# A convolution and two-layer MLP kernel: another layout for two early parts of x, the first convolution by token halves, four VectorE taps ahead of the weight copies, and moved slots of the second product

## The chip, the cores and the metric

The kernel runs on one core of a Trainium2 chip. The metric is the device time of one execution in microseconds. Beside the time there is one profiled execution with a trace of every engine: TensorE (PE, with its weight loads as PEld), VectorE (DVE), ScalarE (ACT), GpSimd (POOL, which also issues DMAs), and SyncE (SP, which issues DMAs).

## The reference

```python
# x (8, 4096, 192), weight (8, 7), w_in (192, 2048), w_out (2048, 192), all float32
w = softmax(weight, axis=-1)                       # 7 taps for each of 8 heads of 24 channels
y[b, s, c] = sum_k w[head(c), k] * x[b, s - 6 + k, c]      # causal, zeros before s = 0
h = y.reshape(32768, 192) @ w_in
out = maximum(0.01 * h, h) @ w_out
```

## The kernel before

**Layout.** Two of the eight sequences are worked on together (e = 0 and 1). Their channels lie on the partitions, 64 channels of one sequence on partitions 0 to 63 and the same 64 of the other on 64 to 127; 192 channels are three such chunks c = 0, 1, 2. Tokens run along the free dimension. The work goes through `groups`: four half groups of 256 tokens (two blocks of 512, each in two halves), then 30 groups of 512 tokens. Of x, the first 1024 tokens of the first two sequences come in four special parts q = 0 to 3 of 256 tokens; the parts 1 and 2 (`x_rows`, loaded at L145) lie token by token on the partitions, two tokens a partition, token s*128+p as slot s of partition p. TensorE transposes them (`transpose_first`, L167) into one bf16 PSUM tile `t[p, s, c, k]`, and VectorE copies that to the transposed input `xt` (`evac_first`, L195), one copy for each s, 384 elements a partition. Everything after comes by DMA and a DMA transpose.

**The convolution.** For most groups VectorE does it: a first tap at L222 and six multiply-adds at L228 for each chunk, 21 instructions in all (`conv_jobs`). The first group's convolution, and chunks 0 and 2 of the second group's, are matmuls with diagonal weights (`pe_conv_jobs`, L259): the taps as two bf16 parts p = 0 and 1, so 14 jobs a chunk with a matmul for each e, 64 rows by 64 columns of the array. With `cross` the two sequences land on exchanged PSUM halves, so that a crossed chunk and an uncrossed one use different quarters of the array, and four matmuls run at once. `evac` multiplies by the reciprocal of the softmax sum (`rsum`) and brings the result to `yt`; a crossed one takes two instructions of 64 partitions. The diagonals `diag[c][:, p]` are made by VectorE (L420) in the order (0,0), (0,1), (1,0), (2,0), (1,1), (2,1).

In the kernel before, the first group's chunk 0 is split by the parts of the taps: part 0 into `hi`, part 1, crossed, into `low`, which ScalarE scales (L455), and one VectorE instruction (L465) adds both.

**The two products.** `mm1` (L507) is called for u = 0, 1, ...; each call makes one PSUM tile `ph` of 128 by 1024 (two feature chunks of a half group, or one of a 512 group, for both sequences) and a ScalarE Prelu (L515) that writes `g`. There are two `ph` tiles. A half group has eight u in four steps j, a 512 group sixteen in eight steps. In the very first u, chunk 0's and chunk 1's matmuls come first, then the transposes of part 1, then chunk 2's. `w_in` exists on the partitions in two arrangements; `spread_down` (L322) and `spread_up` (L326) copy 64 partitions to the other 64 once a piece has landed, since each sequence needs all weights on its own partitions. Its second half (`w_in[1]`) is needed from u = 4 of the first group on.

The second product of the four half groups is done in **row slots** (`mm2_row_slot`, L525), 256 of them. A pair of output tiles of 128 tokens takes 32 slots in two rounds of 16. A slot is two matmuls, one on each half of the array's rows; in the second round the halves change places. Between the rounds stands a **seal**: at the last slot of the first round ScalarE copies out the other tile of the pair before (`evac_o`, L638), after that round's last matmul, and the first matmuls of the second round wait for this copy:

```python
            if first and rnd == 1:
                sync(ins, seal, "both row tiles have left these banks")
        if last and rnd == 0:
            seal_round(p, ins)
        if last and rnd == 1:
            evac_o(pair[0])
```

With slot number q, q = 16, 48, 80, ... wait for a seal, and q = 32, 64, ... do not.

**What orders the work.** The schedule is written by hand: each engine does its instructions in program order. `plan` says how many row slots follow the two u of each step j of group i, and `between` how many of them are put ahead of the second u (0 ahead of the first and 4 ahead of the second, in the steps listed). Behind the last half group's step 7 the 512 groups use another form of the second product (L588). `CUTS` says behind which u of the first group the second group's convolution matmuls go. VectorE convolves group i+1 while group i is in the products.

Of the kernel before, what the change touches and what calls it, by code (L numbers as in the profile page):

```python
# [10 lines left out]
FP32 = mybir.dt.float32  # L11
# [4 lines left out]
def kernel(  # L16
# [8 lines left out]
    nc = tc.nc  # L25
# [11 lines left out]
    NCH = D // CH  # L37
    ST = 512
    SUB = ST // 128
    HT = ST // 2  # L40
    HS = SUB // 2
# [8 lines left out]
    for k in range(K):  # L50
        SKEW += [(2, k), next(pair)]
    SKEW += [(1, 5), (0, 6), (1, 6)]
    CUTS = {1: (0, 6), 3: (6, 11), 5: (11, 14)}
    GB = 32
    NR = D // (2 * GB)

    const_pool = ctx.enter_context(tc.tile_pool(name="const", bufs=1))
# [14 lines left out]
    groups = [(b, h * HT, HT) for b in range(NHALF) for h in range(2)]  # L72
# [49 lines left out]
    def new_xt(rp):  # L122
# [10 lines left out]
    x_rows = {  # L133
        q: const_pool.tile([128, 2, HS, D], BF16, name=f"x_rows{q}") for q in (1, 2)
    }

    def load_first(q):
        rows = x[0:2, q * HT : (q + 1) * HT, :].rearrange("e (s p) d -> p e s d", s=HS)
        if q == 0:
            x_nat[q] = stage_pool.tile([128, 2, HS, D], FP32, name="x_nat")  # L140
            for s in range(HS):
                nc.sync.dma_start(out=x_nat[q][:, :, s], in_=rows[:, :, s])
        elif q in x_rows:
            for e in range(2):
                nc.gpsimd.dma_start(out=x_rows[q][:, e], in_=rows[:, e])  # L145
        else:
            for c in range(NCH):
                for e in range(2):
                    nc.gpsimd.dma_start(  # L149
                        out=x_half[q][:, c, :, e, :],  # L150
                        in_=rows[:, e, :, c * CH : (c + 1) * CH],
                    )
# [7 lines left out]
    ptr = {}  # L160

    def transpose_first(q, mid=None):
        if q:
            t = psum_o.tile([128, HS, NCH, 128], BF16, name="ptr", tag="po")
            for s, c in product(range(HS), range(NCH)):
                for e in range(2):
                    nc.tensor.transpose(  # L167
                        out=t[e * CH : (e + 1) * CH, s, c, :],
                        in_=x_rows[q][:, e, s, c * CH : (c + 1) * CH],
                        identity=ident,  # L170
                    )
            ptr[q] = [t[:, s] for s in range(HS)]
            return
        ts = [
            psum_o.tile([128, NCH, 128], FP32, name=f"ptr{s}", tag="po") for s in range(HS)
        ]
        for s, t in enumerate(ts):
            if s and mid is not None:
                mid()
            for c in range(NCH):  # L180
                nc.tensor.matmul(
                    out=t[:, c, :],
                    lhsT=x_half[q][:, c, s, :, :].rearrange("p e k -> p (e k)"),
                    rhs=ident,
                    start=True,
                    stop=True,
                )
        ptr[q] = ts

    def evac_first(q, *copies):  # L190
        dst = xt[0][:, :, HALO + q * HT : HALO + (q + 1) * HT]
        dst = dst.rearrange("p c (s k) -> p s c k", s=HS)
        for s, t in enumerate(ptr.pop(q)):
            for cs in (slice(0, 1), slice(1, NCH)) if q == 0 and s else (slice(0, NCH),):
                copies[s](out=dst[:, s, cs], in_=t[:, cs])  # L195

    def transpose_half(q):
# [37 lines left out]
    def y_of(grp, c):  # L235
        blk, t0, T = grp
        if blk not in yt:
            yt[blk] = yt_pool.tile([128, NCH, ST], BF16, name="yt")
        return yt[blk][:, c, t0 : t0 + T]

    def acc_tile():
        return psum_o.tile([128, ST], FP32, name="acc", tag="po")
# [37 lines left out]
    def run(*lists):  # L280
        for slots in zip_longest(*lists, fillvalue=()):
            for both in slots:
                for job in both:
                    job()
# [27 lines left out]
    near, far = slice(0, WF // 2), slice(WF // 2, WF)  # L312
# [8 lines left out]
    def spread_down(n, copy=nc.vector.tensor_copy, cols=slice(0, WF)):  # L321
        copy(out=w_in[n][0:CH, 1, cols], in_=w_in[n][CH:128, 0, cols])  # L322

    def spread_up(n, slots=slice(0, 3, 2), cols=slice(0, WF)):
        to = slice(slots.start // 2 + 1, (slots.stop - 1) // 2 + 2)
        nc.vector.tensor_copy(out=w_in[n][CH:128, to, cols], in_=w_in[n][0:CH, slots, cols])  # L326
# [121 lines left out]
    load_x(2)  # L448
    diag_wide(1, 1)
    diag_wide(2, 1)  # L450
    spread_up(0, slice(0, 1), near)
    spread_down(0, cols=near)

    def act_scale(out, in_, scale):
        nc.scalar.activation(  # L455
            out=out, in_=in_, func=mybir.ActivationFunctionType.Copy, scale=scale
        )

    hi = acc_tile()
    low = const_pool.tile([128, HT], FP32, name="low")  # L460
    pe_hi, _ = pe_conv_jobs(groups[0], 0, parts=(0,), accs=[hi] * 2)
    pe_lo, evac_lo = pe_conv_jobs(groups[0], 0, cross=True, parts=(1,))
    run(pe_hi, pe_lo)
    evac_lo(act_scale, act_scale, out=low)
    nc.vector.scalar_tensor_tensor(  # L465
        out=y_of(groups[0], 0), in0=hi[:, :HT], scalar=rsum[:, 0, :], in1=low,
        op0=mybir.AluOpType.mult, op1=mybir.AluOpType.add,
    )
    spread_up(0, slice(2, 3), near)
    pe_1, evac_1 = pe_conv_jobs(groups[0], 1)  # L470
    pe_2, evac_2 = pe_conv_jobs(groups[0], 2, cross=True, accs=[acc_tile(), wps[:, 0]])
# [1 line left out]
    evac_1(act_scale)  # L473
    evac_2(nc.vector.tensor_scalar_mul, act_scale)
    spread_up(0, slice(0, 1), far)
    spread_down(0, nc.scalar.copy, far)


    g, po, acc2, osb, seal = {}, {}, {}, {}, None
# [151 lines left out]
    def evac_o(n):  # L631
# [18 lines left out]
    plan = {  # L650
        0: [0] * 4,
        NSW - 2: [16, 8, 8, 16],
        NSW - 1: [8, 8, 16, 16],
        NSW: [16, 8, 8, 16, 8, 8, 16, 16],
    }
    between = {(1, 0): (3, 5)}
    for i, js in ((NSW - 2, (2, 3)), (NSW - 1, (1, 2)), (NSW, (2, 3, 5, 6))):
        between.update({(i, j): (0, 4) for j in js})
    slot = 0

# [9 lines left out]
    for i, grp in enumerate(groups):  # L670
        blk, t0, T = grp
        steps = T // 64
        if t0 == 0:
            g[blk] = g_pool.tile([128, NFC, 2, ST], BF16, name="g", tag="g")
        quota = plan.get(i, [16] * 4 if T == HT else [5, 5, 6, 5, 5, 6, 8, 8])

        if i == 0:
            ahead = []
        else:
            ahead = conv_jobs(groups[i + 1]) if i + 1 < len(groups) else []  # L680
        per = -(-len(ahead) // steps)
        for j in range(steps):
            early = between.get((i, j), (0, 0))
            for u in range(2 * j, 2 * j + 2):
                mm2_slots(i, early[u % 2])
                mm1(grp, u, 128 if i <= NSW else CH)
                if i == 0 and u == 0:
                    evac_first(1, nc.vector.tensor_copy, nc.vector.tensor_copy)
                    spread_up(0, slice(2, 3), far)
                    conv_1 = conv_jobs(groups[1], (1,))  # L690
                    run([conv_1[:3]])
                    spread_down(1)
                    spread_up(1, slice(0, 1), near)
                    spread_up(1, slice(2, 3))
                    run([conv_1[3:5]])
                    spread_up(1, slice(0, 1), far)
                    run([conv_1[5:]])
                    pe_0, evac_0 = pe_conv_jobs(groups[1], 0)
                    pe_2, evac_2 = pe_conv_jobs(groups[1], 2, cross=True)
                if i == 0 and u in CUTS:  # L700
                    cut = slice(*CUTS[u])
                    run(pe_0[cut], pe_2[cut])
                if i == 0 and u == 5:
                    evac_0(nc.vector.tensor_scalar_mul)
                    evac_2(nc.vector.tensor_scalar_mul, nc.vector.tensor_scalar_mul)
                if i == 0 and u == 6:
                    transpose_first(2)
                    evac_first(2, nc.vector.tensor_copy, nc.vector.tensor_copy)
            jobs = ahead[per * j : per * (j + 1)]
            if T == ST:  # L710


                jobs = ahead[len(ahead) * j // steps : len(ahead) * (j + 1) // steps]
                for job in jobs:
                    job()
                jobs = []
            mm2_slots(i, quota[j] - sum(early))
            if i == 1 and j == 1:
                load_x(3, transpose_x(2))
            for job in jobs:  # L720
                job()
            if i == 0 and j == 3:
                transpose_half(3)

            last_half = t0 + T == ST
            if i == NSW and j == steps - 1:
                evac_o(LAST - 1)
                slot = NSW * NR * NFC
            if j == steps // 4 and last_half and blk > 0:
                load_x(blk + 3)  # L730
            if j == steps // 2 and last_half and blk > 0:
                transpose_x(blk + 2)
# [35 lines left out]
```

## Time and profile before

| | |
|---|---|
| median of 3 runs | 681.26 us (680.83 to 681.55) |
| the profiled execution, first to last instruction | 679.2 us |
| the median less that span | 2.06 us |
| granted TensorE clock, mean of the core | 1.000 |
| VectorE busy, ScalarE busy | 481.2 us (71%), 517.6 us (76%) |
| DMA, mean over the span | 78 GB/s |

The first 17 us are a start-up, in which DMAs, diagonals, copies of weights and the first convolutions must come before products can run. From 17 to 64 us the half groups run with row slots, from there the 512 groups, and 128 matmuls of the last group end the program. In the timeline a row gives the start, the time to the end of the last instruction in it, and the group; matmuls overlap, so the time from one row's start to the next row's start is what a block took. Times below count from the first instruction.

### The profile page before, as it was taken

The page shows a single profiled execution, that of the slowest core. Times are in us where ns is not written, and L with a number is a line of the kernel's source. Part 1 is how long each engine was busy: PE and PEld are TensorE (multiplying, and loading weights), DVE is VectorE, ACT ScalarE, POOL GpSimd, SP SyncE. Part 2 cuts the span into 40 slices and gives each one's busy share as a digit, 9 for nine tenths or more (in the row PEclk, how much of TensorE's full clock was granted, in tenths as well). Part 3 has the DMA queues.
Part 4 walks back from the last instruction along what each step waited for, and adds up shares of the span by engine and source line. Part 5 has one row for each costly group of instructions (what it writes and reads, how often), then busy time and mean ns, then how long its engine had stood idle before and what let it go on. Part 6 is the DMA issues. An engine that isn't in the chain of part 4 may idle for free.

```text
span 679.2 us, 27092 instructions
## 1 busy us (share of the span) xinstructions
PE 674.9 (99%) x12442; PEld 446.3 (66%) x12442; DVE 481.2 (71%) x816; ACT 517.6 (76%) x601; POOL 147.4 (22%) x208
## 2 busy tenths in 40 slices
PE   9999999999999999999999999999999999999998
PEld 6997666666666666666666666666666666666667
DVE  7989477866768766778667687667786676876612
ACT  7899877777787777777777777778777777777781
POOL 8455221122211222211222112222022220000000
PEclk9999999999999999999999999999999999999999
DMA  9999755655737656556556566567365573321123
GB/s 149 99 119 104 52 85 83 84 64 67 96 74 93 76 54 86 84 85 86 66 63 92 80 92 78 56 83 94 73 87 69 60 96 71 72 56 33 34 49 94
DMA packets 213970, 53.27 MB, mean 78 GB/s; under 512 B 209312, under 2 KB 213536, under 8 KB 213856
## 3 DMA queue, kind: packets, MB, share of 16 engines
q0 software_dynamic: 98832, 13.97, 30.3%
q1 hardware_dynamic: 115008, 37.57, 28.0%
q8 instruction: 97, 1.59, 0.9%
q14 instruction: 17, 0.14, 0.1%
q10 hardware_dynamic: 16, 0.00, 0.0%
HBM read 28.31 MB, written 25.17 MB: 79 GB/s over the span
## 4 chain that ended last, share of the span: by engine, by line
PE 98%; DVE 1%; ACT 0%; issue 0%; ACTq 0%
PE ph L507 49%; PE acc L588 44%; PE po L525 5%; PE acc L259 0%; DVE diag L420 0%; PE ptr L167 0%; ACT L366 0%; ACTq L288 0%; DVE w_in L322 0%; DVE yt L465 0%; DVE o_sb L638 0%; DVE x_half L155 0%; ACT w L372 0%; DVE w_in L326 0%; ACT junk L366 0%
## 5 line engine op out<-in xcount | busy, mean ns | idle before, releaser
L515 ACT ACTIVATE g<-ph 128x1024 bf16<-128x1024 f32 x512 | 496.6, 1021 | 139.8 <-PE ph L507 139.6
L228 DVE SCALAR_TENSOR_TENSOR yt<-xt,wk,yt 128x512 bf16<-128x512 bf16 (+1 forms) x582 | 380.1, 715 | 0.2
L507 PE MATMUL ph<-yt,w_in 64*64 64x512 bf16 (+2 forms) x6048 | 377.5, 369 | 0.3 <-DVE yt L465 0.3
L588 PE MATMUL acc<-g,w_out 64*64 64x512 bf16 x5568 | 339.9, 376 | 0.0
L507 PEld LDWEIGHTS <-w_in 64*64 64x64 bf16 (+1 forms) x6048 | 229.7, 131 | 103.4 <-issue 1.1
L588 PEld LDWEIGHTS <-w_out 64*64 64x64 bf16 x5568 | 178.2, 118 | 118.8
L96 POOL DMA_DIRECT2D x_bf<-in_x_dram x180 | 133.9, 774 | 407.6 <-DMA xt<-x_bf 405.6
L610 DVE STREAM_TRANSPOSE o_t<-acc 128x512 f32<-128x512 f32 x87 | 72.9, 875 | 182.2 <-PE acc L588 182.2
L525 PE MATMUL po<-w_out,g 64*128 64x192 bf16 (+1 forms) x640 | 36.8, 243 | 0.0
L525 PEld LDWEIGHTS <-g 64*128 64x128 bf16 (+1 forms) x640 | 32.6, 95 | 3.2 <-issue 0.4
L222 DVE TENSOR_SCALAR yt<-xt,wk 128x512 bf16<-128x512 bf16 (+1 forms) x97 | 28.8, 320 | 2.4 <-DMA xt<-x_bf 2.4
L598 ACT COPY junk<-junk 128x1 f32<-128x1 f32 x58 | 11.1, 191 | 4.1
L638 DVE COPY o_sb<-po 128x192 f32<-128x192 f32 x8 | 2.8, 356 | 6.8 <-PE po L525 3.9
L638 ACT COPY o_sb<-po 128x192 f32<-128x192 f32 x16 | 5.1, 323 | 0.3
L259 PE MATMUL acc<-xt,diag 64*64 64x256 bf16 x126 | 4.7, 272 | 0.1
L149 POOL DMA_DIRECT2D x_half<-in_x_dram x6 | 4.3, 732 | 0.9 <-DMA w_in<-in_moe_w_in_dram 0.9
L259 PEld LDWEIGHTS <-diag 64*64 64x64 bf16 x140 | 3.7, 106 | 1.0 <-issue 0.4
L360 PE MATMUL warm<-const-bfloat16-1.0 128*128 128x512 bf16 (+2 forms) x8 | 3.3, 577 | 0.8 <-PEq L752 0.8
L145 POOL DMA_DIRECT2D x_rows<-in_x_dram x4 | 2.9, 746 | 0.0
L316 POOL DMA_DIRECT2D w_in<-in_moe_w_in_dram x5 | 2.9, 593 | 0.0
L360 PEld LDWEIGHTS <-const-bfloat16-1.0 128*128 128x128 bf16 x10 | 1.2, 128 | 2.2 <-issue 2.2
L326 DVE COPY w_in<-w_in 64x512 bf16<-64x512 bf16 (+1 forms) x7 | 2.3, 337 | 0.2
(52 smaller groups left out, 25.9 us busy)
## 6 DMA issues: line engine op xcount, KB each, us to landing
out_dram<-o_t SPq DMA_DIRECT2D x112, 192.0 KB, 4.7
x_bf<-in_x_dram POOLq DMA_DIRECT2D x180, 64.0 KB, 3.1
out_dram<-o_sb SPq DMA_DIRECT2D x8, 192.0 KB, 2.8
xt<-x_bf SPq DMA_TRANSPOSE x90, 3.2
w_out<-in_moe_w_out_dram POOLq DMA_DIRECT2D x2, 384.0 KB, 8.3
out_dram<-o_t SPq DMA_DIRECT2D x8, 96.0 KB, 2.4
out_dram<-o_sb SPq DMA_DIRECT2D x8, 96.0 KB, 1.7
w_in<-in_moe_w_in_dram POOLq DMA_DIRECT2D x2, 256.0 KB, 5.5
```

Source lines behind the costliest of these rows:

```text
L96: ins = nc.gpsimd.dma_start(out=t[:, c, :, e, :], in_=src[2 * rp + e, :, :, c * CH : (c + 1) * CH],)
L222: lambda s=src, d=dst, c=c: nc.vector.tensor_scalar_mul(d, s, wk[:, c, 0:1])
L228: lambda s=src, d=dst, c=c, k=k: nc.vector.scalar_tensor_tensor(out=d, in0=s, scalar=wk[:, c, k : k + 1], in1=d, op0=mybir.AluOpType.mult, ...
L259: lambda k=k, p=p, a=a, ps=ps, to=to, acc=accs[e]: nc.tensor.matmul(out=acc[to, :T], lhsT=diag[c][ps, p, k, :], rhs=xt[0][ps, c, a : a + T ...
L360: nc.tensor.matmul(out=to[:, 0:cols], lhsT=ones[:, 0:128], rhs=ones[:, 0:cols], start=True, stop=True,)
L507: nc.tensor.matmul(out=ph[m : m + M, e, i * T : (i + 1) * T], lhsT=w_in_of(f, e, c, m, m + M), rhs=y[ps, c, t0 : t0 + T], start=(c == chun ...
L515: act = nc.scalar.activation(out=g[blk][:, nf * u : nf * (u + 1), :, t0 : t0 + T], in_=ph.rearrange("p e (i t) -> p i e t", i=nf), func=my ...
L525: return nc.tensor.matmul(out=po[m], lhsT=g[b][ps, fc, e, s * 128 : (s + 1) * 128], rhs=w_out[ps, fc, :], start=start, stop=stop,)
L588: ins = nc.tensor.matmul(out=acc2[gi, r][e * CH : (e + 1) * CH, 0:T], lhsT=w_out_of(ps, fc, r), rhs=g[b][ps, fc, e, t0 : t0 + T], start=fi ...
L598: seal = nc.scalar.copy(out=junk, in_=junk)
L610: nc.vector.transpose(out=osb[gi, 0][:, 0 : T // GB, :, r], in_=acc2.pop((gi, r))[:, 0:T].rearrange("p (j k) -> p j k", k=GB),)
L638: ins = copy(out=o_sb[:, n % 2, :], in_=po.pop(n))
```

## The change

The loads of parts 1 and 2 of x put tokens 2p and 2p+1 on partition p, so that one row of 1536 bytes is fetched for a partition and sequence, where two of 768 bytes were. The PSUM tile keeps its form, and its copy to `xt` reads the slots s as the innermost dimension, chunk 1 first (256 elements), then chunks 0 and 2 (512 elements).

The first group's chunk 0 is convolved in two halves of 128 tokens, both parts of the taps in each, the second half crossed. ScalarE alone brings both to `yt`. The copies of `w_in` come behind in program order, and the copy at the last `spread_down(0, ...)` goes from ScalarE to VectorE.

In the first group VectorE does four taps of the second group's chunk 1 ahead of the copies of `w_in[1]` where it did three; a fifth and a sixth are placed between those copies, and the seventh after the evacuation of chunk 0. The third cut of convolution matmuls and the evacuations come behind u = 4, where they came behind u = 5.

Eight row slots go from group 4 (the first 512 group) to group 3, and `plan` and `between` are set anew for both.

```diff
-    CUTS = {1: (0, 6), 3: (6, 11), 5: (11, 14)}
+    CUTS = {1: (0, 6), 3: (6, 11), 4: (11, 14)}
...
     def load_first(q):
         rows = x[0:2, q * HT : (q + 1) * HT, :].rearrange("e (s p) d -> p e s d", s=HS)
+        if q in x_rows:
+            rows = x[0:2, q * HT : (q + 1) * HT, :].rearrange("e (p s) d -> p e s d", s=HS)
...
     def evac_first(q, *copies):
         dst = xt[0][:, :, HALO + q * HT : HALO + (q + 1) * HT]
+        if q:
+            dst = dst.rearrange("p c (k s) -> p c k s", s=HS)
+            t = ptr.pop(q).rearrange("p s c k -> p c k s")
+            for copy, cs in zip(copies, (slice(1, 2), slice(0, NCH, 2))):
+                copy(out=dst[:, cs], in_=t[:, cs])
+            return
...
-    spread_up(0, slice(0, 1), near)
-    spread_down(0, cols=near)
...
-    hi = acc_tile()
-    low = const_pool.tile([128, HT], FP32, name="low")
-    pe_hi, _ = pe_conv_jobs(groups[0], 0, parts=(0,), accs=[hi] * 2)
-    pe_lo, evac_lo = pe_conv_jobs(groups[0], 0, cross=True, parts=(1,))
-    run(pe_hi, pe_lo)
-    evac_lo(act_scale, act_scale, out=low)
-    nc.vector.scalar_tensor_tensor(
-        out=y_of(groups[0], 0), in0=hi[:, :HT], scalar=rsum[:, 0, :], in1=low,
-        op0=mybir.AluOpType.mult, op1=mybir.AluOpType.add,
-    )
+    blk, t0, T = groups[0]
+    pe_a, evac_a = pe_conv_jobs((blk, t0, T // 2), 0)
+    pe_b, evac_b = pe_conv_jobs((blk, t0 + T // 2, T // 2), 0, cross=True)
+    run(pe_a, pe_b)
+    evac_a(act_scale)
+    evac_b(act_scale, act_scale)
+    spread_up(0, slice(0, 1), near)
+    spread_down(0, cols=near)
     spread_up(0, slice(2, 3), near)
...
     spread_up(0, slice(0, 1), far)
-    spread_down(0, nc.scalar.copy, far)
+    spread_down(0, cols=far)
...
         NSW - 2: [16, 8, 8, 16],
-        NSW - 1: [8, 8, 16, 16],
-        NSW: [16, 8, 8, 16, 8, 8, 16, 16],
+        NSW - 1: [16, 16, 16, 8],
+        NSW: [8, 16, 8, 8, 16, 8, 8, 16],
...
-    for i, js in ((NSW - 2, (2, 3)), (NSW - 1, (1, 2)), (NSW, (2, 3, 5, 6))):
+    for i, js in ((NSW - 2, (2, 3)), (NSW, (0, 1, 3, 4, 6, 7))):
         between.update({(i, j): (0, 4) for j in js})
...
                     conv_1 = conv_jobs(groups[1], (1,))
-                    run([conv_1[:3]])
+                    run([conv_1[:4]])
                     spread_down(1)
                     spread_up(1, slice(0, 1), near)
                     spread_up(1, slice(2, 3))
-                    run([conv_1[3:5]])
+                    run([conv_1[4:5]])
                     spread_up(1, slice(0, 1), far)
-                    run([conv_1[5:]])
+                    run([conv_1[5:6]])
...
-                if i == 0 and u == 5:
+                if i == 0 and u == 4:
                     evac_0(nc.vector.tensor_scalar_mul)
+                    run([conv_1[6:]])
                     evac_2(nc.vector.tensor_scalar_mul, nc.vector.tensor_scalar_mul)
```

More of the change, by code (lines that the diff above doesn't have):

```diff
@@ L171, in transpose_first @@
                     )
-            ptr[q] = [t[:, s] for s in range(HS)]
+            ptr[q] = t
             return
@@ L191, in evac_first @@
         dst = xt[0][:, :, HALO + q * HT : HALO + (q + 1) * HT]
+        if q:
[4 more added lines that the diff above has]
+            return
         dst = dst.rearrange("p c (s k) -> p s c k", s=HS)
         for s, t in enumerate(ptr.pop(q)):
-            for cs in (slice(0, 1), slice(1, NCH)) if q == 0 and s else (slice(0, NCH),):
+            for cs in (slice(0, 1), slice(1, NCH)) if s else (slice(0, NCH),):
                 copies[s](out=dst[:, s, cs], in_=t[:, cs])
```

## The prediction

> **What bounds the kernel now.** I read the page's busy times and chain first, then the waits of TensorE, then the timelines of single stretches.
>
> ```profile
> PE 674.9 (99%) x12442; PEld 446.3 (66%) x12442; DVE 481.2 (71%) x816; ACT 517.6 (76%) x601; POOL 147.4 (22%) x208
> PE 98%; DVE 1%; ACT 0%; issue 0%; ACTq 0%
> ```
>
> TensorE carries the chain; ScalarE and VectorE have a quarter of the span free. Busy time can hide stalls, so I compare block lengths. Two u and 16 slots of a half group take 2.63 us (rows at 19.75, 22.38, 25.01, 27.64), the same each time; six L507 matmuls of 512 columns always take 0.65 and eight slot matmuls 0.33. The view of waits lists none for TensorE from 17 to 63 us. So **from 17 us on TensorE has no slack to give back**: a stall there goes into the time in full, and a gain can only come from before. There the waits are small: from 4 to 17 us I count 2.7 us beyond the pace of the columns (a 256-column group of four matmuls every 0.109 us); nearly half is the change between forms of the array, 0.12 to 0.13 a change, and the diff changes their number by none.
>
> This is a stretch of group 4 with its row slots, TensorE and then ScalarE (start, length, group):
>
> ```profile
> 50.61 0.81 PE L507 MATMUL ph<-yt,w_in 64*128 64x512 bf16 x6
> 51.26 0.50 PE L525 MATMUL po<-w_out,g 64*128 64x192 bf16 x8
> 51.59 0.81 PE L507 MATMUL ph<-yt,w_in 64*128 64x512 bf16 x6
> 52.24 0.49 PE L525 MATMUL po<-w_out,g 64*128 64x192 bf16 x8
> 52.57 0.81 PE L507 MATMUL ph<-yt,w_in 64*128 64x512 bf16 x6
> 53.22 0.50 PE L525 MATMUL po<-w_out,g 64*128 64x192 bf16 x8
> 53.55 0.81 PE L507 MATMUL ph<-yt,w_in 64*128 64x512 bf16 x6
> ```
>
> ```profile
> 49.51 3.96 ACT L515 ACTIVATE g<-ph 128x1024 bf16<-128x1024 f32 x4 [0.33 <-PE ph L507]
> 53.37 0.31 ACT L638 COPY o_sb<-po 128x192 f32<-128x192 f32 x1
> 53.56 1.96 ACT L515 ACTIVATE g<-ph 128x1024 bf16<-128x1024 f32 x2
> ```
>
> See the order on ScalarE. A step "u, 4 slots, u, 4 slots" ends on TensorE at 52.57. Its last Prelu still runs then, so the `evac_o` copy behind it runs from 53.37 to 53.68: **0.80 to 1.11 us after the slots ended**. Today that costs nothing: 52.57 is q = 192, a pair's end (192 = 6 x 32), and nobody waits for that copy soon.
>
> **Moved slots.** Summing the old plan, steps end at q = 112, 144, 176, 208 and 240 (odd multiples of 16, where the next slot waits for the seal) only behind 12 or 16 slots, and two whole u follow: 1.30 us of cover. Q = 176 shows it: slots end at 48.66, the copy runs 48.87 to 49.18, slots go on at 49.95. In the new plan group 3 ends at q = 168. Group 4 then goes u, 4, u, 4 and is at 176; u, 4, u, 12 to 192; u, u, 8 to 200; u, 4, u, 4 to 208; u, 4, u, 12 to 224; u, u, 8 to 232; u, 4, u, 4 to 240; u, 4, u, 12 to 256. So the three seals at 176, 208 and 240 stand behind the short block of 4 slots, and **only one u (0.65 us) stands between a seal and the slots that wait for it**. The steps ahead (u, u, 8, then u, 4, u, 4) are those of the fence, so the copy ends 1.11 us after the block; 0.05 us passes from a ScalarE end to a matmul that waited (5.10 to 5.15). The stall is 1.11 + 0.05 - 0.65 = 0.51 us, three times: **+1.53 us**. Queued behind the waiting matmul on TensorE are 4 slots, a u and 12 slots; ScalarE, the one that could catch up, is not the bound. Bounds: 0.8 us in all if the Prelu ahead starts 0.25 us sooner each time, 1.8 if the weight load also waits (0.1 each). VectorE's convolution of group 4 ends at 46.16, just when group 4 begins (46.04); eight slots more in group 3 move that need 0.66 us later, which covers VectorE's new lateness below. SP's transposes of the next block stand behind an output DMA that comes a step sooner; VectorE waited 1.67 us for them at 47.82 and will wait less, and none of that is on the path.
>
> **Chunk 0 by halves.** It goes from 28 matmuls of 256 columns to 56 of 128: 14 groups of four. Nearest row: the transposes (L167), 12 matmuls of 128 columns in 0.46 us, a pair every 0.055, each with 64 weight columns. So 14 x 0.056 = 0.78 us, as long as now (5.15 to 5.93); slow end, one group for each 0.106 us weight load of L259: 1.5 us, 0.6 late for all behind. I take the fast end: the transposes load weights at that pace. [...]
> Two ScalarE instructions (0.95) and one on VectorE (0.48) go; three on ScalarE come. L455 takes 0.47 for 256 columns, and 128 columns fewer are 0.11 less (L195 on ScalarE: 0.48, 0.38, 0.27 for 384, 256, 128), so 3 x 0.37 from 6.14, when `rsum` is there: chunk 0 is ready at 7.25, where it was at 8.04. What is late next is chunk 1:
>
> ```profile
> 7.70 0.47 ACT L455 ACTIVATE yt<-acc,rsum 128x256 bf16<-128x256 f32 x1 [0.49 <-PE acc L259]
> 8.20 0.47 ACT L455 ACTIVATE yt<-wps,rsum 64x256 bf16<-64x256 f32 x1
> 8.70 0.62 ACT L322 COPY w_in<-w_in 64x512 bf16<-64x512 bf16 x1
> ```
>
> Its matmuls wait for the diagonal (2,0), done at 5.97, in both kernels, so they still end at 7.65 and this row still runs 7.70 to 8.18. Chunk 0's products start at 7.70 instead of 8.09, but chunk 1's at 8.23 instead of 8.31: **only 0.08 us won**. ScalarE's weight copy (0.62) goes to VectorE (0.29 to 0.55); ScalarE's next work waits for TensorE anyway.
>
> **VectorE up to the weight copies.** It loses L465 and gets the far copy, so `evac_first(1)` starts at about 9.2 (9.22 now; the transposes end at 9.1). Its two copies read with a stride now. Fast end: the present rate, 384 elements in 0.35 (0.65 for both, start to next start). Slow end, one element at a time, from copies of 4-byte PSUM elements: 96 in 0.247 (L409), 192 in 0.358 (L638), 1.15 ns an element, so 256 in 0.43 and 512 in 0.73; less 0.08 of overlap each, 1.0. I take the slow end: a strided 2-byte element is read alone like those. [...] No row here shows such a copy. Then comes the fourth tap (0.52) ahead of the copies of `w_in[1]`:
>
> ```profile
> 12.21 0.42 DVE L322 COPY w_in<-w_in 64x1024 bf16<-64x1024 bf16 x1 [0.61 <-DMA w_in<-in_moe_w_in_dram]
> 12.64 0.77 DVE L326 COPY w_in<-w_in 64x512 bf16<-64x512 bf16 x2
> ```
>
> Third tap's end now 11.59, plus 0.37 for the copies, plus 0.52: VectorE is free at 12.48, the idle 0.61 is gone, and the copies begin 0.27 later than now (0.0 with fast copies). The DMA does not decide: half as many rows and a cheaper POOL issue (0.57 for 64 rows in L316, 0.74 for 256 in L145) bring the weights no later than 12.2. What waits are u = 4's matmuls: they start at 13.01, and the last weight copy ends at 13.41, 0.05 before TensorE takes it at 13.47; that is on the path. So u = 4 is 0.27 late.
>
> **Cut and taps.** The cut (0.33 and two form changes, as now) goes between u = 4 and u = 5. ScalarE has Prelu 4 at 14.39 (14.13 now) but Prelu 5 waits for a u behind the cut: 15.70, where 15.05 was. Prelu 6 and 7 follow it at 0.92, u = 7 waits for Prelu 5's tile until 16.77 (16.44 now), and group 1 starts at 17.69 instead of 17.37. Group 1's last piece of `yt` is done at 17.1 instead of 17.2 and needed at 17.9. `evac_first(2)` costs 0.37 too; group 2's convolution ends near 25.9, needed at 27.6. The start-up's sum: **+0.32 us**; with fast copies 0.0, with slow copies of weights beside POOL's issues +0.6.
>
> **Sum.** The profiled span 679.2 + 0.32 + 1.53 = 681.05; with the 2.06 between it and the median of the runs, 683.1. About 0.2% (1.36 us) is what a measurement of this kernel can tell from no change: faster is under 679.90, slower over 682.62.
>
> **Rivals.**
> 1. *The seals do not bind* (not slower). ScalarE would have to end the copy within 0.65 us of the block, so start the Prelu ahead 0.46 us sooner than in the fence; from there the stall is nothing. For it: stalls on TensorE let ScalarE catch up. Against: that Prelu starts 0.2 us behind its own u, so it can't. Time 681.26 + 0.32 = 681.6. Chance 0.13.
> 2. *Weight loads set the pace of the halves*: chunks 1 and 2 start 0.6 late, and VectorE's chain with them; 683.1 + 0.6 = 683.7. For it: L259's loads are as long as its groups. Against: L167. Chance 0.08.
> 3. *The start-up gains*: copies at the present rate, weights at 11.8, and 0.5 won; 681.26 - 0.5 + 1.53 = 682.3. Against: chunk 1's wait for its diagonal. Chance 0.07. With no seal stall it would give 680.8; even all the waits before 17 us, 1.3 without the form changes, do not reach faster.
>
> The forecast has 0.72; its own range, by the bounds above, is 682.4 to 683.7. The range takes in the first rival and stops short of the worst of the second: 681.6 to 683.9. Slower: 0.72 and 0.08, less 0.04 for the forecast's low edge, 0.76. Faster 0.02 (all of the start-up won and no stall). The rest, 0.22, is within 0.2%.
>
> **What would show it.** Group 4's timeline should have three places where, behind a seal copy at +0.8 to +1.1 us, L525 starts about 1.16 us after the block and not 0.65, and a wait of L525 for ScalarE's L638. The L195 copies should take about 0.43 and 0.73, `spread_down(1)` start at 12.5 without idle time before it, and group 1's first u at 17.7. I am wrong if L525 in group 4 goes without gaps, or if group 1 starts before 17.2.

## The result and the profile after

| | before | after |
|---|---|---|
| median of 8 runs each, same chip | 681.18 us (680.78 to 681.61) | 683.02 us (682.59 to 683.36) |
| ratio, 95% interval | | 1.0028 (1.0019 to 1.0037) |
| the profiled execution's span | 679.2 us | 680.9 us |

The change makes the kernel 0.28% slower. The prediction said 683.1, in a range of 681.6 to 683.9. The page of the kernel after, part 1 (busy time of each engine), part 4 (the chain that ended last, by engine) and one group of part 5 (busy time and mean ns of one, then idle time ahead of it and what ended most of it), and the same group before:

```profile
PE 675.8 (99%) x12470; PEld 446.5 (66%) x12470; DVE 481.9 (71%) x816; ACT 517.7 (76%) x601; POOL 146.5 (22%) x208
PE 98%; ACT 2%; DVE 0%; issue 0%; ACTq 0%
L528 PE MATMUL po<-w_out,g 64*128 64x192 bf16 (+1 forms) x640 | 37.0, 243 | 1.0 <-ACT o_sb L641 1.0
```

```profile
L525 PE MATMUL po<-w_out,g 64*128 64x192 bf16 (+1 forms) x640 | 36.8, 243 | 0.0
```

Busy times and counts hardly move (28 matmuls more, all in the first chunk's convolution). What is new is in the other lines: ScalarE is on the chain with 2%, and the slot matmuls (L525 before, L528 now) sat idle 1.0 us for ScalarE's copy of the row tiles (L638 before, L641 now). The view of TensorE's waits from 17 to 66 us has only this line (total, times, longest); before, the same view is empty:

```profile
PE po L528 <- ACT o_sb L641: 1.0, 3, 0.4
```

The timelines of the kernel after around the first of the three, TensorE and then ScalarE (start, time to the end of the row's last instruction, group, and in brackets the idle time before it):

```profile
48.52 0.51 PE L528 MATMUL po<-w_out,g 64*128 64x192 bf16 x8
48.89 0.84 PE L510 MATMUL ph<-yt,w_in 64*128 64x512 bf16 x6
50.03 0.51 PE L528 MATMUL po<-w_out,g 64*128 64x192 bf16 x8 [0.29 <-ACT o_sb L641]
50.37 0.81 PE L510 MATMUL ph<-yt,w_in 64*128 64x512 bf16 x6
```

```profile
45.80 3.96 ACT L518 ACTIVATE g<-ph 128x1024 bf16<-128x1024 f32 x4 [0.29 <-PE ph L510]
49.66 0.31 ACT L641 COPY o_sb<-po 128x192 f32<-128x192 f32 x1
49.86 1.04 ACT L518 ACTIVATE g<-ph 128x1024 bf16<-128x1024 f32 x1
```

The block of four slots ends at 48.89. The seal's copy starts 0.77 us later, behind the Prelus, and ends at 49.97, 1.08 after the block. One u of 0.65 lies between, and the next slots start at 50.03, not at 49.54. The bracket says only 0.29, because idle time is counted from the modelled end of the last matmul; the start-to-start time, 1.14 where six such matmuls take 0.65, is the honest measure. The other two seals look the same: L510 rows at 55.92 and 62.97, slots again at 57.08 and 64.13. Summed over whole blocks against their undisturbed length, TensorE lost 0.54, 0.53 and 0.53 us, **1.59 us in all**.

The start-up, in the timeline of the kernel after, VectorE and then TensorE (`...` stands for rows left out):

```profile
9.21 1.02 DVE L198 COPY xt<-ptr 128x256 bf16<-128x256 bf16 x2 [0.23 <-PE ptr L169]
10.26 0.29 DVE L334 COPY w_in<-w_in 64x512 bf16<-64x512 bf16 x1
10.58 0.37 DVE L230 TENSOR_SCALAR yt<-xt,wk 128x256 bf16<-128x256 bf16 x1
10.99 1.53 DVE L236 SCALAR_TENSOR_TENSOR yt<-xt,wk,yt 128x256 bf16<-128x256 bf16 x3
12.55 0.42 DVE L330 COPY w_in<-w_in 64x1024 bf16<-64x1024 bf16 x1
12.98 0.62 DVE L334 COPY w_in<-w_in 64x512 bf16<-64x512 bf16 x2
```

```profile
10.28 0.85 PE L267 MATMUL acc<-xt,diag 64*64 64x256 bf16 x24
...
13.17 1.11 PE L510 MATMUL ph<-yt,w_in 64*128 64x256 bf16 x12
14.22 0.52 PE L267 MATMUL acc<-xt,diag 64*64 64x256 bf16 x12
...
17.57 0.83 PE L510 MATMUL ph<-yt,w_in 64*128 64x256 bf16 x12
```

The same copies and the start of group 1 in the kernel before, VectorE and TensorE:

```profile
9.22 0.62 DVE L195 COPY xt<-ptr 128x384 bf16<-128x384 bf16 x2
...
17.37 0.82 PE L507 MATMUL ph<-yt,w_in 64*128 64x256 bf16 x12
```

The strided copies take 1.02 us (0.62 before), the copies of `w_in[1]` start at 12.55 with no idle time before them (12.21 before, after 0.61 of idle time), and group 1 starts at 17.57 (17.37 before): **the start-up lost 0.20 us** in this pair of profiles. 0.20 and 1.59 make 1.79. The first matmul of the other form of the second product (L588 before, L591 now) starts at 67.55, where it started at 65.77, 1.78 later, and the spans, given to a tenth, differ by 1.7.

### The profile page after: what moved, and what is told of

It is laid out like the page before. It is cut to its first block, busy times and chain, and to the rows that moved or that the text cites. A ratio compares the mean times of both kernels' runs of the same rounds, so it can differ in the third digit from the quotient of the medians.

```text
span 680.9 us, 27148 instructions
## 1 busy us (share of the span) xinstructions
PE 675.8 (99%) x12470; PEld 446.5 (66%) x12470; DVE 481.9 (71%) x816; ACT 517.7 (76%) x601; POOL 146.5 (22%) x208
## 3 DMA queue, kind: packets, MB, share of 16 engines
q8 instruction: 97, 1.59, 1.0%
## 4 chain that ended last, share of the span: by engine, by line
PE 98%; ACT 2%; DVE 0%; issue 0%; ACTq 0%
PE ph L510 48%; PE acc L591 44%; PE po L528 4%; ACT g L518 1%; PE acc L267 1%; PE warm L368 0%; DVE xt L198 0%; PE ptr L169 0%; ACT o_sb L641 0%; PE ptr L183 0%; ACT yt L460 0%; PE wps L267 0%; DVE o_sb L641 0%; PE wps L368 0%; PE wps L404 0%
## 5 line engine op out<-in xcount | busy, mean ns | idle before, releaser
L510 PE MATMUL ph<-yt,w_in 64*64 64x512 bf16 (+2 forms) x6048 | 378.0, 369 | 0.2 <-ACT yt L460 0.2
L591 PE MATMUL acc<-g,w_out 64*64 64x512 bf16 x5568 | 339.9, 376 | 0.0
L510 PEld LDWEIGHTS <-w_in 64*64 64x64 bf16 (+1 forms) x6048 | 229.8, 131 | 103.1 <-issue 1.3
L591 PEld LDWEIGHTS <-w_out 64*64 64x64 bf16 x5568 | 178.2, 118 | 118.8
L528 PE MATMUL po<-w_out,g 64*128 64x192 bf16 (+1 forms) x640 | 37.0, 243 | 1.0 <-ACT o_sb L641 1.0
L528 PEld LDWEIGHTS <-g 64*128 64x128 bf16 (+1 forms) x640 | 32.7, 95 | 5.2 <-ACT o_sb L641 2.4
L601 ACT COPY junk<-junk 128x1 f32<-128x1 f32 x58 | 11.1, 191 | 4.1
L641 DVE COPY o_sb<-po 128x192 f32<-128x192 f32 x8 | 2.8, 357 | 6.8 <-PE po L528 4.6
L641 ACT COPY o_sb<-po 128x192 f32<-128x192 f32 x16 | 5.0, 319 | 0.3
L267 PE MATMUL acc<-xt,diag 64*64 64x256 bf16 (+1 forms) x154 | 4.7, 252 | 0.1
L267 PEld LDWEIGHTS <-diag 64*64 64x64 bf16 x168 | 3.8, 106 | 1.0 <-issue 0.6
L460 ACT ACTIVATE yt<-acc,rsum 64x128 bf16<-64x128 f32 (+2 forms) x4 | 1.6, 391 | 1.2 <-PE acc L267 0.8
```

The costliest lines, as they stand in the source:

```text
L267: lambda k=k, p=p, a=a, ps=ps, to=to, acc=accs[e]: nc.tensor.matmul(out=acc[to, :T], lhsT=diag[c][ps, p, k, :], rhs=xt[0][ps, c, a : a + T ...
L510: nc.tensor.matmul(out=ph[m : m + M, e, i * T : (i + 1) * T], lhsT=w_in_of(f, e, c, m, m + M), rhs=y[ps, c, t0 : t0 + T], start=(c == chun ...
L528: return nc.tensor.matmul(out=po[m], lhsT=g[b][ps, fc, e, s * 128 : (s + 1) * 128], rhs=w_out[ps, fc, :], start=start, stop=stop,)
L591: ins = nc.tensor.matmul(out=acc2[gi, r][e * CH : (e + 1) * CH, 0:T], lhsT=w_out_of(ps, fc, r), rhs=g[b][ps, fc, e, t0 : t0 + T], start=fi ...
L601: seal = nc.scalar.copy(out=junk, in_=junk)
L641: ins = copy(out=o_sb[:, n % 2, :], in_=po.pop(n))
```

## The experiments

The theory: three stalls at the seals, +1.5 to 1.6 us, and a start-up that is a few tenths late because of the strided copies. The main rival: the start-up carries the loss (copies, taps, cut), and the waits at the seals would be given back. A second question came from the trace: whether the parts that should gain (the halves, the taps) gain anything, and whether a plan without the stalls lets them.

Each kernel was timed in five rounds beside the kernel before on the same chip, the kernels of one batch together (e1 to e4, e5 to e8, e9 to e12). "Difference" is the mean of all its runs less the mean of all runs of before in its batch, with a 95% interval. The ratio and its interval are the recorded ones; the quotient of the plain medians can differ from them (for e12 it is 1.0013). In a single profile the start-up varies: the first convolution started between 5.00 and 5.48 us, in no order by kernel, and the first piece of `w_in[1]`, with the loads as before, had landed between 11.5 and 13.0. So the start of group 1 in one profile is good to some tenths only, and the differences decide.

| kernel | median | ratio (95%) | difference, us |
|---|---|---|---|
| e1, change with the old slots | 681.41 | 1.0006 (0.9997 to 1.0015) | +0.35 ± 0.22 |
| e2, the new slots alone | 682.75 | 1.0026 (1.0016 to 1.0036) | +1.65 ± 0.21 |
| e3, change, u pairs unsplit behind the seals | 682.60 | 1.0023 (1.0014 to 1.0033) | +1.47 ± 0.26 |
| e4, e1 with the old layout and copies | 681.37 | 1.0006 (0.9997 to 1.0014) | +0.26 ± 0.31 |
| e5, the layout and copies alone | 681.50 | 1.0008 (0.9999 to 1.0017) | +0.38 ± 0.22 |
| e6, the taps and the cut alone | 681.07 | 0.9998 (0.9990 to 1.0007) | -0.10 ± 0.24 |
| e7, the halves alone | 681.37 | 1.0003 (0.9994 to 1.0012) | +0.18 ± 0.25 |
| e8, halves, copies shared with ScalarE | 681.38 | 1.0003 (0.9994 to 1.0012) | +0.20 ± 0.21 |
| e9, halves with a third plan | 681.26 | 1.0001 (0.9992 to 1.0010) | +0.22 ± 0.23 |
| e10, halves, taps, cut, third plan | 681.39 | 1.0003 (0.9994 to 1.0012) | +0.36 ± 0.26 |
| e11, the third plan alone | 681.40 | 1.0002 (0.9993 to 1.0011) | +0.28 ± 0.23 |
| e12, change with the third plan | 681.99 | 1.0008 (0.9999 to 1.0017) | +0.74 ± 0.21 |

### The slots: e1, e2, e3

**e1**, the change with the plan of before:

```diff
-        NSW - 1: [16, 16, 16, 8],
-        NSW: [8, 16, 8, 8, 16, 8, 8, 16],
+        NSW - 1: [8, 8, 16, 16],
+        NSW: [16, 8, 8, 16, 8, 8, 16, 16],
...
-    for i, js in ((NSW - 2, (2, 3)), (NSW, (0, 1, 3, 4, 6, 7))):
+    for i, js in ((NSW - 2, (2, 3)), (NSW - 1, (1, 2)), (NSW, (2, 3, 5, 6))):
```

> The changed kernel with the slot plan of before. Theory: the three seals that wait cost 1.6 us and the start-up 0.2. So L528 waits for no L641 copy, group 1 still starts near 17.57 us, the span is 679.3 (680.9 in the changed kernel) and the time 681.4. Rival: the slots cost for another reason, or the start-up carries the loss; then the time stays at 682.5 or more.

**e2**, the kernel before with only the new plan, so the same lines the other way round:

> The kernel before with nothing but the new slot plan. Theory: 681.2 + 1.6 = 682.8, with three waits for the seal copy at q = 176, 208 and 240, each some 0.53 us, and group 1 at 17.37 as before. Rival: if the loss needs the start-up's parts, the time stays at 681.2.

**e3**, the change, but in the steps whose second u stands behind a seal's block both u go together, with all eight slots behind them:

```diff
-    for i, js in ((NSW - 2, (2, 3)), (NSW, (0, 1, 3, 4, 6, 7))):
+    for i, js in ((NSW - 2, (2, 3)), (NSW, (0, 3, 6))):
```

> The changed kernel, but the three steps behind a seal are not split: two u stand before their slots. Theory: 1.30 us cover the seal copy's 1.16, so no slot waits for a seal; but the second u waits for its ph tile, which the Prelu behind the short block gives back 0.95 us after the block where u comes at 0.65, 0.30 each. Span 680.9 - 1.6 + 0.9 = 680.2, time 682.3. Rival one: only the split matters, 681.4. Rival two: it is not the seal, 683.0.

Measured: e1 +0.35, e2 +1.65, and the whole change +1.80 ± 0.28 in its own batch. Nearly the whole loss comes and goes with the plan. e2's waits of TensorE, 17 to 66 us (total, times, longest), and two rows of its TensorE timeline:

```profile
PE po L525 <- ACT o_sb L638: 1.0, 3, 0.3
```

```profile
49.01 0.84 PE L507 MATMUL ph<-yt,w_in 64*128 64x512 bf16 x6
50.14 0.50 PE L525 MATMUL po<-w_out,g 64*128 64x192 bf16 x8 [0.29 <-ACT o_sb L638]
```

These are the three stalls of the change, without its start-up: 0.53, 0.53 and 0.53 us by block lengths, 1.58 in all, beside a measured 1.65 ± 0.21. e1 has no wait for a seal. So the rival, that the start-up carries the loss, falls.

e3 shows what stands beside the seal. With two u between a seal and its next slots the wait for L641 is gone, but the second u needs the tile that ScalarE has yet to read (TensorE's timeline of e3):

```profile
49.14 0.51 PE L528 MATMUL po<-w_out,g 64*128 64x192 bf16 x8
49.51 1.76 PE L510 MATMUL ph<-yt,w_in 64*128 64x512 bf16 x12
51.08 1.51 PE L528 MATMUL po<-w_out,g 64*128 64x192 bf16 x32
```

Twelve such matmuls take 1.30; from 49.51 to 51.08 it is 1.57. With the 0.04 in the block ahead 0.31 is lost, and 0.33 at each of the other two, 0.97 where 0.9 was expected. The lateness of ScalarE, a u of 1.0 us of Prelu for 0.65 of TensorE, is paid in one form or the other in both plans; slots are TensorE work that asks nothing of ScalarE, and where 12 or 16 of them stand ahead of a seal and two u behind it (before, e1) neither form shows. The time of e3 is 682.6 where 682.3 was expected. The 0.97 and e1's +0.35 for the rest of the change make 1.32, and the measured +1.47 ± 0.26 agrees with that.

### The parts of the start-up: e4 to e7

**e4**, e1 with the old layout, `load_first`, `ptr` and `evac_first` as in the kernel before; **e5**, the reverse, the kernel before with only these:

```diff
+        if q in x_rows:
+            rows = x[0:2, q * HT : (q + 1) * HT, :].rearrange("e (p s) d -> p e s d", s=HS)
...
-            ptr[q] = [t[:, s] for s in range(HS)]
+            ptr[q] = t
...
+        if q:
+            dst = dst.rearrange("p c (k s) -> p c k s", s=HS)
+            t = ptr.pop(q).rearrange("p s c k -> p c k s")
+            for copy, cs in zip(copies, (slice(1, 2), slice(0, NCH, 2))):
+                copy(out=dst[:, cs], in_=t[:, cs])
+            return
```

> The changed kernel with the old slots, the old layout of parts 1 and 2 of x and the old copies (left of the change: halves of tokens, four taps, the cut behind u = 4). Theory: the strided copies cost the start-up its 0.2 us, first because the first cut of convolution matmuls waits for the PSUM tile that they read. So the first cut starts at 10.1 instead of 10.28, the weight copies at 12.2, group 1 at 17.4, and the time is 0.2 under the run with old slots alone, 681.2. Rival: the cut between u = 4 and u = 5 costs it; then group 1 stays at 17.55.

> The kernel before with the new layout of parts 1 and 2 of x and the strided copies alone. Theory: the two copies take 1.02 us from start to end instead of 0.62, and the first cut of convolution matmuls, which reads what they write, starts 0.15 to 0.2 later than in the kernel before; the three taps still end before 12.1, so the weight copies hardly move. Group 1 starts 0.1 to 0.2 later, time 681.2 to 681.3. Rival: the start-up's loss comes from the tap and the cut; then 681.1.

e4's first cut of convolution matmuls started at 10.05, without the wait that the change has there (10.28). But in its profile a piece of `w_in` kept VectorE waiting 0.48 us at 10.37, and group 1 started at 17.95. Its difference, +0.26 ± 0.31, can't be told from e1's, and 681.2 was expected; e4 decides nothing. e5 has the wait. TensorE's timeline in e5, the first cut and the start of group 4:

```profile
10.38 0.85 PE L267 MATMUL acc<-xt,diag 64*64 64x256 bf16 x24
...
46.53 0.41 PE L515 MATMUL ph<-yt,w_in 64*128 64x512 bf16 x2 [0.24 <-DVE yt L236]
47.19 1.06 PE L515 MATMUL ph<-yt,w_in 64*128 64x512 bf16 x8 [0.25 <-DVE yt L236]
```

The cut waited 0.19 us for VectorE's second copy, which writes chunks 0 and 2 of `xt`, the data that these matmuls read. (Where an expectation puts this down to a tile in PSUM, that is not the cause.) Group 1 started only 0.09 late. The larger price came 29 us later: VectorE has almost no idle time between 17 and 46 us (0.07 in e5), so what `evac_first` adds twice, 0.40 each time, stays in its chain, and so does the 0.19 by which the first convolution started later in that profile (0.99 together). Group 4's convolution ended at 47.14, where it ended at 46.16 before, and group 4 starts at 46.04 in the kernel before. TensorE lost 0.84 us there in this profile; over all runs e5 is +0.38 ± 0.22.

**e6**, the kernel before with only the taps and the cut:

```diff
-    CUTS = {1: (0, 6), 3: (6, 11), 5: (11, 14)}
+    CUTS = {1: (0, 6), 3: (6, 11), 4: (11, 14)}
...
-                    run([conv_1[:3]])
+                    run([conv_1[:4]])
...
-                    run([conv_1[3:5]])
+                    run([conv_1[4:5]])
...
-                    run([conv_1[5:]])
+                    run([conv_1[5:6]])
...
-                if i == 0 and u == 5:
+                if i == 0 and u == 4:
                     evac_0(nc.vector.tensor_scalar_mul)
+                    run([conv_1[6:]])
```

> The kernel before with the fourth tap and the cut behind u = 4 alone. Theory: with copies at the old rate the tap fits the idle time ahead of the weight copies (0.61 us before), so these start near 12.2 as before, and Prelu 5, though 0.4 later, costs less than 0.1 at group 1: time 681.1 to 681.2. Rival: the cut's place costs 0.2 to 0.3 by itself, 681.35 or more.

Measured -0.10 ± 0.24: no change that can be told. The weight copies started at 12.16, right behind the fourth tap, beside 12.21 before. (In this execution their load had landed by 11.46, ahead of the third tap's end at 11.61, so the tap and not the load held them; beside the kernel before that cost nothing, because there VectorE waited for the load until 12.2.) Prelu 5, 0.23 us later than before (15.28 for 15.05), made nobody late: group 1 started at 17.28.

**e7**, the kernel before with only the halves (and the order of the `w_in` copies that goes with them):

```diff
+    pe_a, evac_a = pe_conv_jobs((blk, t0, T // 2), 0)
+    pe_b, evac_b = pe_conv_jobs((blk, t0 + T // 2, T // 2), 0, cross=True)
+    run(pe_a, pe_b)
+    evac_a(act_scale)
+    evac_b(act_scale, act_scale)
...
-    spread_down(0, nc.scalar.copy, far)
+    spread_down(0, cols=far)
```

> The kernel before with the first chunk by token halves alone. Theory: the first product starts at 7.7 instead of 8.1, but chunk 1's, behind its evacuation, near 8.3 as before, so nothing is won behind it: time 681.1. Rival: the earlier start is kept, 680.7.

Measured +0.18 ± 0.25, where 681.1 was expected (it is 681.37). In its profile group 1 started at 17.09, 0.28 sooner; the first convolution had started 0.15 sooner in that execution (5.00 for 5.15). But group 4 waited for VectorE's convolution again: 0.60 us were lost from 44.44 on, and the convolution ended at 46.53, though the start-up was sooner. VectorE had one wait of 0.6 us there for the load of an early part of x (L222 in the view of its waits); without it its chain would have ended near 45.9 (an estimate), sooner than before. So in this execution a gain of TensorE was lost where it met VectorE's chain, and that one wait is enough to explain it; that it would be lost in every execution is not shown.

### Looking for a version that keeps the gains: e8 to e12

**e8** is e7 with the new layout; the transposes of part 1 go behind chunk 0's products, and ScalarE takes chunk 1's strided copy, VectorE the one of chunks 0 and 2 (the removal of `evac_first(1, ...)` from its old place is left out here):

```diff
-            if wide and (i, c) == (0, 2):
+            if wide and (i, c) == (0, 1):
                 transpose_first(1)
+                evac_first(1, nc.scalar.copy, nc.vector.tensor_copy)
```

> A version made from the theory: old slots, three taps and the old cuts; halves of tokens; the transposes of part 1 of x put behind chunk 0's products, where TensorE waits for chunk 1; the new layout, with chunk 1's strided copy on ScalarE while VectorE does chunks 0 and 2. Theory: the wait of 0.35 us ahead of chunk 1's products is filled, the weight copies start at 11.5 to 11.8, group 1 starts 0.3 to 0.5 sooner than 17.37: time 680.6 to 680.8. Rival: the DMA of w_in sets the pace of the start-up anyway, 681.1.

It fell short: 681.38, +0.20 ± 0.21, where 680.6 to 680.8 was expected. VectorE's timeline of e8 shows a wait that the sharing brings in:

```profile
9.76 0.69 DVE L198 COPY xt<-ptr 128x512 bf16<-128x512 bf16 x1 [0.25 <-ACT xt L198]
10.48 0.29 DVE L334 COPY w_in<-w_in 64x512 bf16<-64x512 bf16 x1
```

VectorE's copy waited for ScalarE's, which stood behind ScalarE's evacuations of chunks 1 and 2, and ended at 10.45, where the two on VectorE ended at 10.23 in the change. But the first convolution started 0.33 late in that profile, at 5.48, which is more than this difference, so that the wait is what cost the gain is not shown.

**e9, e10, e11 and e12** have a third plan, with 16 slots in every step of group 3, so that group 4 starts later still for VectorE, and with two u behind the block of every seal (the lines removed are those of the change):

```diff
-        NSW - 1: [16, 16, 16, 8],
-        NSW: [8, 16, 8, 8, 16, 8, 8, 16],
+        NSW - 1: [16, 16, 16, 16],
+        NSW: [8, 8, 16, 8, 8, 16, 8, 8],
...
-    for i, js in ((NSW - 2, (2, 3)), (NSW, (0, 1, 3, 4, 6, 7))):
+    for i, js in ((NSW - 2, (2, 3)), (NSW, (1, 2, 4, 5, 7))):
```

e9 is e7 with it, e10 is e9 with e6's edits, e11 the kernel before with it, e12 the change with it.

> Halves of tokens alone, and sixteen slots moved from group 4 to group 3, so that the seal at q = 176 stands behind 16 slots and those at 208 and 240 behind 12, each with two u after it. Theory: with halves alone group 1 started 0.28 sooner, and 0.60 was lost again where group 4's first u waits for VectorE's convolution; 1.3 us more in group 3 take that wait away, no seal binds, and the gain stays: 680.7 to 680.9. Rival: the halves gain nothing, the start in that profile was chance; then 681.2.

> The run before and the fourth tap with the cut behind u = 4 (old layout and copies). Theory: as taps and cut alone cost nothing that shows (681.07 beside 681.21), they add between -0.1 and +0.1: 680.6 to 681.0. Rival: they collide with the sooner start, 681.2.

> The kernel before with sixteen slots moved to group 3 and no other edit. Theory: moving slots costs nothing by itself when every seal has two u behind it; no wait of the slots for a seal copy, group 4's start without a wait for VectorE: 681.1 to 681.2, 1.6 under the run with the new slot plan alone. Rival: slots in group 3 instead of group 4 cost by themselves; then some 0.8 to 1.6 over that.

> The changed kernel, all parts of it, with this slot plan in place of its own. Theory: the three stalls of 0.53 us go and nothing else changes: 683.0 - 1.6 = 681.4, less 0.1 for the wait at group 4's start that the run with the old slots still had. Rival: the loss is bound to the parts of the start-up together with any move of slots; then 682.5 or more.

None of the four waits for a seal, and none stalls at group 4's start. e12 takes back 1.06 of the 1.80 us, less than the 1.7 expected: it is at 681.99, where 681.3 was expected. e9 and e10 were expected below 681 and are not. e11 shows a part of the reason: the third plan has a price of its own, +0.28 ± 0.23, where next to nothing was expected. TensorE's timeline of e12 at the end of the slots:

```profile
64.36 0.84 PE L510 MATMUL ph<-yt,w_in 64*128 64x512 bf16 x6
65.01 0.53 PE L528 MATMUL po<-w_out,g 64*128 64x192 bf16 x8
65.46 1.72 PE L510 MATMUL ph<-yt,w_in 64*64 64x512 bf16 x24
66.96 0.38 PE L591 MATMUL acc<-g,w_out 64*64 64x512 bf16 x1
```

Before, group 4 ends with 16 slots in one block, and the next 24 matmuls took 1.35 us (64.42 to 65.77); here only four slots stand there, ScalarE is a u behind, and they take 1.50: the 13th of them starts at 66.32, 0.05 after group 4's last Prelu ended at 66.27. With 0.03 to 0.05 behind group 4's first slots and some 0.03 ahead of the 24, this plan loses 0.21 to 0.22 us against the old one from group 1's start to the first L588 matmul (L583 and L591 in the others), in e9, e10, e11 and e12 alike. With e1's +0.35 that makes 0.56, and e12's +0.74 ± 0.21 agrees with it. Taken off, e9 is 0.00 and e10 +0.14, each good to some 0.3: the halves, with or without the taps, win nothing that these runs can tell, as the rival in e9's expectation had it. **No version here beats the kernel before.**

## Why the prediction was right

Point by point, in the prediction's order.

- **TensorE has no slack from 17 us on.** Shown: the three stalls of e2, 1.58 us by its profile, are in the time in full, +1.65 ± 0.21.
- **Moved slots, +1.53.** Right in place, cause and size: 1.59. The copy ended 1.08 to 1.10 us after the block in the place of 1.11, and 0.06 passed to the matmul in the place of 0.05. The small rest is around the wait: the slots behind it ran 0.01 longer, and the block ahead of the first seal 0.04. The weight loads of the slots wait for the same copy (2.4 us of idle time in the page's row of them), which may be why; no run separates it. Rival 1, that the seals do not bind, is excluded by the three waits.
- **The eight slots as cover for VectorE at group 4.** Right, and worth more than its half sentence. In the change VectorE's convolution ended at 46.48 and group 4 started at 46.90. With the old plan (e1) group 4 started at 46.46 and that chain ended at 46.74; TensorE lost 0.12 in that profile. So the moved slots do pay for the new layout there; they cost several times as much at the seals. The aside on the next block's transposes was half right: VectorE's first wait for them was no shorter (1.75 us up to 48.23, 1.67 before), only a second one of 0.71 was gone. Neither cost anything.
- **Chunk 0 by halves.** The 14 groups of four ran every 0.056 us, as taken from the transposes; rival 2, the weight loads, fell. Chunk 0 was ready at 7.39 and not at 7.25, still ahead of its products. First products at 7.71 (7.70 predicted), chunk 1's at 8.30 (8.23; 8.31 before): won 0.01 where 0.08 was predicted, since chunk 1's evacuation started 0.08 later than in the profile of before.
- **The strided copies.** 0.424 and 0.678 us, predicted 0.43 and 0.73 from the 1.15 ns an element of the copies of 4-byte elements; from the one copy to the other it is 0.99 ns. That a strided element is read alone was the author's reading: the rows show the times, not the reason. The fast end fell, and with it rival 3.
- **A term that was not in the sum.** The first cut of convolution matmuls waits for the second strided copy: 10.28, where it was 10.11. It hardly adds, as the next thing that TensorE waits for, the weight copies, is late for the same reason; it did not spoil the sum.
- **Weight copies at 12.48, u = 4 late by 0.27.** Measured 12.55, and its matmuls end about as late as predicted (Prelu 4 at 14.32 for 14.39). Prelu 5 came at 15.56, not 15.70, half of it from there and half from the cut (1.24 us from Prelu 4 to Prelu 5, predicted 1.31), and group 1 at 17.57, not 17.69. e6 agrees that the cut is cheap: cut and taps alone cost nothing that can be told. The start-up's +0.32 was thus +0.20 in that profile. That this comes so close is in part luck: group 1 started at 17.37, 17.69 and 18.19 in the three profiles with the start-up of before (before, e2, e11) and at 17.57, 17.79, 18.18 and 18.34 in the four with the change's (after, e1, e3, e12). Over many runs it is in the +0.35 ± 0.22 of e1, which has group 4's stall in it too. That the DMA does not decide was right as well: with the new layout the first piece of `w_in[1]` had landed by 10.5 to 11.7 us in six profiles (after, e1, e3, e5, e8, e12), with the old one by 11.5 to 13.0 in eight. The new rows do bring the weights some 0.7 us sooner (medians 11.1 and 11.9), but in the change VectorE, with the longer copies and the fourth tap ahead, comes for them at 12.5. For the high end of the start-up's sum, +0.6 with weight copies slow beside POOL's issues, no run shows the cause: in the change VectorE's copies of 512 elements took 0.29 to 0.39 us with POOL's DMA issues beside them, and before, 0.29 (at 6.67) and 0.55 (at 6.97) stand beside the same L145 issues (6.64 to 8.12).
- **Sum.** 681.05 for the profiled span, 680.9 measured; 683.1 for the median, 683.02 measured. e2 confirms the 1.53 for the seals by itself. That the whole agrees to 0.1 us is finer than the start-up's spread allows and is in part luck.

What stays open: how the +0.2 to 0.4 us outside the slots divide. e5 puts the strided copies first (+0.38 ± 0.22) and e6 and e7 leave nothing to the taps and little to the halves, but the four intervals overlap, e4 did not separate from e1, and part of e5's price lies at group 4 and not in the first 17 us.

## What to carry to other kernels

In a hand-written order, look for each wait at the two numbers that decide it: how long after its block the releasing engine is done, and how much work lies between. Splitting a step more finely puts less work between, and a wait that had been covered for free turns up in full if the waiting engine is the bound (1.58 us in e2's profile, +1.65 ± 0.21 in its time). An engine that fills its time to the last tenth (VectorE here, with 0.07 us idle from 17 to 46 us in e5) is a second bound: a gain of the first can be lost again where the two meet (0.84 us in e5's profile, 0.60 in e7's), so a change to the start is judged at that meeting, not at its own end.

## What the runs showed of the hardware

- A group of four 64 by 64 matmuls of 128 columns, one in each quarter of the array, ran every 0.056 us, though each carried its own weight load of 0.106 us (L267 in the change, mean), and in the kernel before a group of 256 columns ran every 0.109 us. So the loads were wholly covered at half the former column count.
- Reading bf16 from PSUM with a stride cost VectorE 0.424 us for 256 elements a partition and 0.678 for 512 (L198 in the change), so 0.99 ns an element and 0.17 us a copy; the plain copy of 384 elements took 0.35 (L195 before). ScalarE took 0.37 for the strided 256 in e8, less than VectorE's 0.425 there.
- The loads of `x` and `w_in` landed in 16 parts each in these traces, and the last of them was at times far behind the rest. For the first piece of `w_in[1]` 15 had landed by 10.36 us in the profile of before and the last at 12.19; in e11 it was 13.01, and VectorE sat idle 1.44 us for it; in the six other profiles with the same loads the last was 0.4 us behind or less. VectorE's idle 0.61 us ahead of its weight copies, in the profile that the prediction read, is so in part an accident of that execution, and a gain that rests on such a wait should be looked for in several.
